# Attention with a gated MLP on one core: the reciprocals spread by VectorE instead of two DMAs, and the last exponential cut in halves

## The chip, the cores and the metric

One NeuronCore of a Trainium2 chip runs the kernel. Its engines work from queues of their own: TensorE (PE, matrix products), VectorE (DVE), ScalarE (ACT, here mainly exponentials), GpSimd (POOL) and SyncE (SP, which here issues most DMAs). They meet at semaphores. The metric is the device time of one execution in microseconds. The kernel before took 1224.72 us as the median of three executions (1223.39 to 1226.02).

## The reference

The input x has 2048 rows of 512. All is bfloat16.

```python
xn = layernorm(x)                                  # rows of 512
q  = (xn @ wq) as 32 heads of 128
p  = softmax(q @ k_cache.T * 128**-0.5)            # per head, 2048 x 2048
s  = concat(p @ v_cache) @ wo                      # 4096 -> 512
h  = relu(xn @ w1 + b1)**2                         # 512 -> 1792
out = x + s * silu(h @ w2 + b2)
```

Each of the 32 heads has its own 2048 keys and values of 128 numbers. The softmax is computed without subtracting a maximum: the exponentials are summed, and the output of a head is divided by the sum at the end.

## The kernel before

The 2048 query rows are worked in four blocks of 512. A block and a head make a unit g (128 of them: 32 heads for each block in turn), and a unit has eight steps, so there are 1024 steps (`pi`), each over 256 keys. A step computes transposed scores: `gen_scores` makes two products of 128 keys x 512 queries into `psA` (two buffers of 1024 columns), and ScalarE makes one exponential over both, into the tile `pT` (eight buffers). Two steps later the step's products with V follow, into `psO` (two banks). Between scores and V products TensorE runs one or two products of other work, from a list of jobs: projections of q for later heads, the MLP, and the output projection with `wo`, which go through the two banks of `psF` and are evicted by VectorE.

The products with V come in two kinds. In the first (`gen_pv`), pieces of 128x128 of `pT` are the stationary operand and V moves past them, with a column of ones added, so that the denominator comes out as a 129th column; 64 products of 128x129 make a head. VectorE evicts the result (`o_un`), takes the reciprocal, GpSimd scales, and a transposing DMA writes `oT`. In the second (`gen_pv_b`), V is stationary and `pT` moves; 16 products of 128x512 make a head, the result is already transposed, and ScalarE evicts it to `o_col`. The denominator then has to be found beside TensorE: GpSimd adds the two halves of a `pT` tile (`h_sum`) and VectorE reduces it with a transposing reduction (`d_part`), or VectorE reduces the `pT` tile alone at about twice the length. The partial sums of a head are summed (`d_sum`), turned in blocks of 32 (`d_row`), written to memory (`d_scr`), read back (`d_quad`), totalled and inverted (`d_rec`, on 32 partitions). The inverses are written to memory again (`r_scr`) and read back broadcast to all 128 partitions (`r_all`, two buffers). GpSimd multiplies `o_col` by `r_all` into `oT`.

Each engine's order is written out while the kernel is built. The class `_Sched` keeps a clock for each engine from a cost per instruction (`_cost`) and per DMA (`_ISSUE`). VectorE's necessary work (evictions) is placed when it arises; the rest waits in the list `quiet` with a due step, and `fill_dve` puts it wherever the planned clock leaves room. `fill_pool` does the same for GpSimd, and takes reductions off VectorE by placing an `h_sum`; `fill_sync` places the DMAs of the denominators. `ready_at` adds an allowance (`SLACK`, 1500 ns, `HALF_SLACK`, 600 ns) before what waits for a DMA or for an `h_sum`; `POOL_OWED` keeps GpSimd from taking a reduction when VectorE owes little. For each unit, `choose` takes the second kind, unless VectorE's owed work (`owed`) is above `OWED` or no `o_col` buffer of the `NOC` is in sight; the first three and last three units are always of the first kind. In the program as built, units 0-2, 33, 64, 75, 97 and 125-127 are of the first kind.

At the end of a query block `acc_gate` (the line of `_stt`, 249) multiplies the accumulated output by the gate on VectorE, four times a block. After the last unit, `tail_one` runs what is left of the output projection; the very last row tile is written from a buffer of its own, `x_t`, in pieces.

Lines of helpers carry the profile's names: L226 and L231 are the products (L231 those of the first kind), L235 ScalarE's activations, L239 tensor-tensor, L249 the fused form with a scalar, L253 copies, L257 reciprocals, L282 reductions, L286 transposing reductions, L290 the transpose in blocks of 32, L294 and L298 DMAs.

## Time and profile before

| what | value |
|---|---|
| median of three executions | 1224.72 us |
| profiled execution: time, span | 1224.72 us, 1222.9 us |
| granted TensorE clock | 1.000 |
| busy: TensorE, VectorE, ScalarE, GpSimd | 1206.5, 1083.0, 1090.7, 1066.4 us |
| exponentials | 1024, 1026 ns each |
| h_sum additions on GpSimd | 764, 1164 ns each |
| transposing reductions of h_sum, of pT | 764 of 679 ns, 180 of 1209 ns |
| scalings of o_col on GpSimd | 118, 1283 ns each, idle before them 33.5 us |
| DMA to landing: d_scr, d_quad, r_scr, r_all | 2.9, 3.3, 3.2, 3.8 us |

The page's busy time counts an engine's records without their overlap. A group's line gives the source line, engine, operation, tile written and tiles read, count, then busy time, mean length of one and the idle time of the engine just before. Products are pipelined, so their spacing is read from the starts in the timeline and not from their lengths. About one product's record in fifty is missing from the trace; a gap of 0.05 us marked "issue" in TensorE's timeline is such a place.

### The profile page before, as it was taken

To read this page: it belongs to the slowest core of one execution; us is meant where nothing else is said; L and a number is where in the kernel's file an instruction comes from. 1 tells how busy PE (TensorE), PEld (TensorE's weight loads), DVE (VectorE), ACT (ScalarE), POOL (GpSimd) and SP (SyncE) were. 2 spreads that over 40 slices of the span, in tenths; PEclk is the share of its full clock that TensorE was granted. 3 is DMA by queue.
4 is the path that set the end of the run, shared out by engine and by line. 5 is a ranking of instruction groups with operands and counts; after the bars stand their busy time and mean duration, and the time that the engine had idled before them with its cause. 6 is when DMAs were issued, how large, how long until landed. Compare 5 with 4: busy or idle time off the path is not lost.

```text
span 1222.9 us, 19101 instructions
## 1 busy us (share of the span) xinstructions
PE 1206.5 (99%) x6103; PEld 574.9 (47%) x6221; DVE 1083.0 (89%) x1874; ACT 1090.7 (89%) x1162; POOL 1066.4 (87%) x979
## 2 busy tenths in 40 slices
PE   9999999999999999999999999999999999999998
PEld 7544444444444444444454454444445444444445
DVE  4798989899999988889999988888998999988983
ACT  7899999998888999999999999998998899989984
POOL 1689999999788999999988879989898899999981
PEclk9999999999999999999999999999999999999999
DMA  9999997787787887887777898787879788878871
GB/s 217 203 236 195 207 210 148 156 172 151 166 166 153 170 186 150 152 170 157 172 168 159 168 159 174 150 166 167 167 147 158 165 176 161 155 155 159 166 153 49
DMA packets 679300, 203.53 MB, mean 166 GB/s; under 512 B 650881, under 2 KB 662913, under 8 KB 679201
## 3 DMA queue, kind: packets, MB, share of 16 engines
q1 hardware_dynamic: 677104, 198.25, 80.9%
q0 software_dynamic: 1424, 3.81, 1.0%
q8 instruction: 49, 0.80, 0.3%
q14 instruction: 51, 0.41, 0.1%
q10 hardware_dynamic: 672, 0.26, 0.1%
HBM read 128.50 MB, written 4.27 MB: 109 GB/s over the span
## 4 chain that ended last, share of the span: by engine, by line
PE 79%; DVE 14%; POOL 3%; DMA 2%; issue 1%; ACT 1%; ACTq 0%; SPq 0%; POOLq 0%; DVEq 0%
PE psA L226 29%; PE psO L226 27%; PE psF L226 20%; DVE d_part L286 8%; POOL h_sum L239 3%; PE psO L231 2%; DVE acc L249 2%; DMA d_quad<-d_scr 1%; DVE qt_sb L253 1%; DVE d_sum L282 1%; ACT pT L235 0%; DVE acc L239 0%; DVE g_all L249 0%; DMA r_scr<-d_rec 0%; POOL oT L239 0%
## 5 line engine op out<-in xcount | busy, mean ns | idle before, releaser
L235 ACT ACTIVATE pT<-psA 128x1024 bf16<-128x1024 f32 x1024 | 1036.1, 1026 | 111.8 <-PE psA L226 74.2
L239 POOL TENSOR_TENSOR h_sum<-pT 128x512 f32<-128x512 bf16 x764 | 865.1, 1164 | 48.5 <-ACT pT L235 23.6
L226 PE MATMUL psA<-qt_sb,kT 128*128 128x512 bf16 x1980 | 593.3, 379 | 4.3 <-ACT pT L235 1.2
L226 PE MATMUL psO<-pT,v_sb 128*128 128x512 bf16 x1851 | 553.5, 379 | 1.9
L286 DVE TRANSPOSE_TENSOR_REDUCE d_part<-h_sum 128x16 f32<-128x512 f32 x764 | 501.8, 679 | 34.0 <-POOL h_sum L239 32.5
L226 PEld LDWEIGHTS psA<-qt_sb,kT 128*128 128x128 bf16 x2032 | 195.1, 98 | 225.9 <-ACT pT L235 6.8
L226 PEld LDWEIGHTS psO<-pT,v_sb 128*128 128x128 bf16 x1888 | 184.7, 98 | 222.2 <-issue 0.7
L286 DVE TRANSPOSE_TENSOR_REDUCE d_part<-pT 128x32 f32<-128x1024 bf16 x180 | 217.0, 1209 | 5.7 <-ACT pT L235 5.2
L239 POOL TENSOR_TENSOR oT<-o_col,r_all 128x512 bf16<-128x512 f32 x118 | 151.3, 1283 | 33.5 <-DMA r_all<-r_scr 32.0
L226 PE MATMUL psF<-xnT,wq_sb 128*128 128x512 bf16 (+1 forms) x513 | 167.1, 374 | 1.5 <-DVE acc L239 0.6
L226 PE MATMUL psF<-wo_all,oT 128*128 128x512 bf16 x468 | 160.3, 379 | 1.5 <-DVE z_t L249 0.8
L253 DVE CAST qt_sb<-psF 128x512 bf16<-128x512 f32 (+1 forms) x130 | 85.6, 659 | 21.9 <-PE psF L226 19.9
L226 PEld LDWEIGHTS psF<-xnT,wq_sb 128*128 128x128 bf16 x520 | 50.3, 98 | 61.0 <-issue 1.4
L226 PE MATMUL psF<-xnT,w_sb 128*128 128x512 bf16 x219 | 75.7, 379 | 2.1 <-DVE h2T L249 2.0
L226 PEld LDWEIGHTS psF<-wo_all,oT 128*128 128x128 bf16 x480 | 46.9, 98 | 58.3 <-DVE z_t L249 1.3
L226 PE MATMUL psF<-w_sb,h2T 128*128 128x512 bf16 x219 | 72.4, 379 | 0.2
L235 ACT ACTIVATE o_col<-psO 128x512 f32<-128x512 f32 x118 | 69.8, 592 | 0.0
L245 DVE TENSOR_SCALAR r_t<-psF,b1f 128x512 bf16<-128x512 f32 x56 | 40.8, 728 | 12.0 <-PE psF L226 11.3
L231 PEld LDWEIGHTS psO<-v_sb,pT 128*128 128x128 bf16 x640 | 42.4, 98 | 17.6 <-ACT pT L235 0.6
L231 PE MATMUL psO<-v_sb,pT 128*128 128x129 bf16 x640 | 49.0, 220 | 0.3 <-ACT pT L235 0.3
L282 DVE TENSOR_REDUCE d_sum<-d_part 128x16 f32<-128x160 f32 (+3 forms) x118 | 46.6, 395 | 1.5
L249 DVE SCALAR_TENSOR_TENSOR h2T<-psF,b1f,r_t 128x512 bf16<-128x512 f32 x56 | 41.8, 747 | 1.7
(65 smaller groups left out, 383.4 us busy)
## 6 DMA issues: line engine op xcount, KB each, us to landing
v_sb<-in_A_v_cache_dram SPq DMA_DIRECT2D x127, 512.0 KB, 4.8
r_all<-r_scr SPq DMA_DIRECT2D x118, 256.0 KB, 3.8
wq_sb<-in_A_wq_dram SPq DMA_DIRECT2D x127, 128.0 KB, 3.4
wo_all<-in_A_wo_dram SPq DMA_DIRECT2D x4, 1024.0 KB, 5.8
w_sb<-in_B_w_dram SPq DMA_DIRECT2D x14, 256.0 KB, 4.1
x_t<-in_A_x_dram POOLq DMA_DIRECT2D x16, 128.0 KB, 3.4
kT<-in_A_k_cache_dram SPq DMA_TRANSPOSE x127, 5.1
d_scr<-d_row SPq DMA_DIRECT2D x118, 16.0 KB, 2.9
```

The source lines that it names most:

```text
L226: return e.matmul(out, lhsT, rhs, start=start, stop=stop)
L231: return e.matmul(out, lhsT, rhs, start=start, stop=stop, skip_group_check=True)
L235: return e.activation(out, in_, func, bias=bias, scale=scale)
L239: return e.tensor_tensor(out, in0, in1, op)
L245: return e.tensor_scalar(out, in0, scalar1=scalar1, scalar2=scalar2, op0=op0, op1=op1)
L249: return e.scalar_tensor_tensor(out=out, in0=in0, scalar=scalar, in1=in1, op0=op0, op1=op1)
L253: return e.tensor_copy(out, in_)
L282: return e.tensor_reduce(out, in_, axis=AX.X, op=ALU.add)
L286: return e.tensor_reduce(out, in_, axis=AX.X, op=ALU.add, apply_transpose=True)
```

## The change

Three things change together.

- The reciprocals are spread by VectorE. `d_sum` is written straight to memory in another order, every one of the 128 partitions reads the sums of all four groups of 32 rows (`d_quad`), totals and inverts them (`d_rec`), and one VectorE transpose in blocks of 32, whose source repeats each inverse 32 times, writes `r_all` (`den_spread`). `r_all` has one buffer. The turn `d_row`, the write to `r_scr` and the broadcast read go.
- The planner's numbers: `OWED` 9000, three `o_col` buffers, no allowance before `h_sum` reductions and before the scaling, no `POOL_OWED`. The memory saved or used: four buffers for the rows under normalization, a buffer of its own for the warm-up products.
- The last exponential is two of 512 columns, and the last V products are ordered by key half, the first four waiting for the first half alone.

```diff
           "wo_all": (1700, 7200), "w1_sb": (600, 5000), "w2_sb": (700, 5000), "d_scr": (530, 2200),
-          "d_quad": (530, 4200), "r_scr": (530, 2200), "r_all": (1230, 4400)}
+          "d_quad": (1230, 4200)}
...
-    OWED = 8000
-    POOL_OWED = 3500
-    HALF_SLACK = 600
+    OWED = 9000
...
-    NSL, NSW, NQS, NPT, NOT, NOC, NHS = 3, 4, 3, 8, 3 * HC, 4, 3
+    NSL, NSW, NQS, NPT, NOT, NOC, NHS = 3, 4, 3, 8, 3 * HC, 3, 3
...
-    d_sum = sb("d_sum", [P, 2, 32], F32)
-    d_row = sb("d_row", [P, 2, 32], F32)
+    d_sum = sb("d_sum", [P, 2, NBK], F32)
     d_quad = sb("d_quad", [P, 2, 4, NBK], F32)
     d_rec = sb("d_rec", [P, 2, NBK], F32)
-    r_all = sb("r_all", [P, 2, QB], F32)
-    d_scr = nc.dram_tensor("d_scr", [2, P, 32], F32, kind="Internal").ap()
-    r_scr = nc.dram_tensor("r_scr", [2, QB], F32, kind="Internal").ap()
+    r_all = sb("r_all", [P, NBK, 32], F32)
+    d_scr = nc.dram_tensor("d_scr", [2, 32, 4 * NBK], F32, kind="Internal").ap()
...
-    warm = o_bf[:, 0, 0, :]
+    warm = sb("warm", [P, P], BF16)
...
-        t_exp[pi] = E(AC, partial(_act, out=pT[:, pi % NPT, :],
-                                  in_=psA[:, s2 * 1024:(s2 + 1) * 1024],
-                                  func=ACT.Exp, scale=SM_SCALE),
-                      deps=[t, t_PV[pi - NPT] if pi >= NPT else None, t_part.get(pi - NPT)])
-
+        cuts = [0, QB, 2 * QB] if pi == NPAIR - 1 else [0, 2 * QB]
+        for c0, c1 in zip(cuts, cuts[1:]):
+            t_exp[pi] = E(AC, partial(_act, out=pT[:, pi % NPT, c0:c1],
+                                      in_=psA[:, s2 * 1024 + c0:s2 * 1024 + c1],
+                                      func=ACT.Exp, scale=SM_SCALE),
+                          deps=[t, t_PV[pi - NPT] if pi >= NPT else None, t_part.get(pi - NPT)])
+            t_exp0.setdefault(pi, t_exp[pi])
+
+    t_exp0 = {}
...
     def den_sum(g):
         m = b_no[g]
-        t_sum[m] = E(DV, partial(_reduce, out=d_sum[:, m % 2, 0:NBK],
+        t_sum[m] = E(DV, partial(_reduce, out=d_sum[:, m % 2, :],
                                  in_=d_part[:, m % 2, 0:len(t_parts[g]), :].rearrange(
                                      "p n b -> p b n")),
-                     deps=t_parts[g] + [t_row.get(m - 2) if m >= 2 else t_sum0])
-
-    def den_turn(g):
-        m = b_no[g]
-        t_row[m] = E(DV, partial(_transpose32, out=d_row[:, m % 2, :], in_=d_sum[:, m % 2, :]),
-                     deps=[t_sum[m], t_dw.get(m - 2)])
+                     deps=t_parts[g] + [t_dw[m - 2] if m >= 2 else None])
 
     def den_write(g):
         m = b_no[g]
-        t_dw[m] = S.emit_dma(SP, partial(_dma, out=d_scr[m % 2], in_=d_row[:, m % 2, :]),
-                             sl_dw[m % 2], deps=[t_row[m], t_dr.get(m - 2)])
+        dst = bass.AP(tensor=d_scr.tensor, offset=d_scr.offset + m % 2 * P * NBK,
+                      ap=[[NBK, 4], [4 * NBK, 32], [1, NBK]])
+        t_dw[m] = S.emit_dma(SP, partial(_dma, out=dst, in_=d_sum[:, m % 2, :]), sl_dw[m % 2],
+                             deps=[t_sum[m], t_dr[m - 2] if m >= 2 else None])
 
     def den_read(g):
         m = b_no[g]
-        src = bass.AP(tensor=d_scr.tensor, offset=d_scr.offset + m % 2 * P * 32,
-                      ap=[[NBK, 32], [32 * 32, 4], [1, NBK]])
-        t_dr[m] = S.emit_dma(SP, partial(_dma, out=d_quad[0:32, m % 2], in_=src), sl_dr[m % 2],
-                             deps=[t_dw[m], t_tot.get(m - 2)])
+        src = bass.AP(tensor=d_scr.tensor, offset=d_scr.offset + m % 2 * P * NBK,
+                      ap=[[0, 4], [4 * NBK, 32], [1, 4 * NBK]])
+        t_dr[m] = S.emit_dma(SP, partial(_dma, out=d_quad[:, m % 2].rearrange("p a b -> p (a b)"),
+                                         in_=src), sl_dr[m % 2],
+                             deps=[t_dw[m], t_tot[m - 2] if m >= 2 else None])
 
     def den_total(g):
         m = b_no[g]
-        t_tot[m] = E(DV, partial(_reduce, out=d_rec[0:32, m % 2, :],
-                                 in_=d_quad[0:32, m % 2].rearrange("p a b -> p b a")),
-                     deps=[t_dr[m], t_rw.get(m - 2)])
+        t_tot[m] = E(DV, partial(_reduce, out=d_rec[:, m % 2, :],
+                                 in_=d_quad[:, m % 2].rearrange("p a b -> p b a")),
+                     deps=[t_dr[m], t_spr.get(m - 2)])
 
     def den_recip(g):
         m = b_no[g]
-        t_rec[m] = E(DV, partial(_recip, out=d_rec[0:32, m % 2, :], in_=d_rec[0:32, m % 2, :]),
+        t_rec[m] = E(DV, partial(_recip, out=d_rec[:, m % 2, :], in_=d_rec[:, m % 2, :]),
                      deps=[t_tot[m]])
 
-    def rec_write(g):
+    def den_spread(g):
         m = b_no[g]
-        t_rw[m] = S.emit_dma(
-            SP, partial(_dma, out=r_scr[m % 2].rearrange("(p b) -> p b", b=NBK),
-                        in_=d_rec[0:32, m % 2, :]),
-            sl_rw[m % 2], deps=[t_rec[m], t_spr.get(m - 2)])
-
-    def rec_read(g):
-        m = b_no[g]
-        src = bass.AP(tensor=r_scr.tensor, offset=r_scr.offset + m % 2 * QB,
-                      ap=[[0, P], [1, QB]])
-        t_spr[m] = S.emit_dma(SP, partial(_dma, out=r_all[:, m % 2, :], in_=src), sl_rr[m % 2],
-                              deps=[t_rw[m], t_scale.get(m - 2)])
+        base = d_rec[:, m % 2, :]
+        spread = bass.AP(tensor=base.tensor, offset=base.offset,
+                         ap=[list(base.ap[0]), [1, NBK], [0, 32]])
+        t_spr[m] = E(DV, partial(_transpose32, out=r_all[:], in_=spread),
+                     deps=[t_rec[m], t_scale[m - 1] if m else None])
 
     def den_scale(g):
         m = b_no[g]
         t_scale[m] = tok_oT[g] = E(
             GP, partial(_tt, out=oT[:, g % NOT, :], in0=o_col[:, m % NOC, :],
-                        in1=r_all[:, m % 2, :], op=ALU.mult),
+                        in1=r_all[:].rearrange("p b i -> p (b i)"), op=ALU.mult),
             deps=[t_col[m], t_spr[m], t_wodone[g - NOT] if g >= NOT else None])
...
-              den_turn: 110}
+              den_spread: 600}
...
-        calm(first + NPR + 6, partial(den_turn, g))
...
-        sync_quiet.append(partial(rec_write, g))
-        sync_quiet.append(partial(rec_read, g))
+        calm(first + NPR + 13, partial(den_spread, g))
         pool_quiet.append(partial(den_scale, g))
...
-        slack = SLACK if fn.func in (den_total, den_read, rec_read, den_scale) else (
-            HALF_SLACK if fn.func is part_half else 0)
+        slack = SLACK if fn.func in (den_total, den_read) else 0
...
-            if (x < NHS or t_half[x - NHS] is not None) and owed(now[0]) > POOL_OWED:
+            if x < NHS or t_half[x - NHS] is not None:
...
+        if pi == NPAIR - 1:
+            order = [x for n in range(2) for x in order if x[1] == 2 * k + n]
...
-            inc = idx == len(order) - 1 or (last and g > 0 and idx == 3)
+            inc = idx == len(order) - 1 or (last and g > 0 and idx == (5 if g == NG - 1 else 3))
...
-                  deps=[t_exp[ps], t_v0[k % 2] if g == 0 else t_vfill[g], t_ones,
+                  deps=[(t_exp0 if tt == 2 * k else t_exp)[ps], t_v0[k % 2] if g == 0 else t_vfill[g], t_ones,
```

## Prediction

> **What bounds the kernel now.** I read the page first, then TensorE's waits, then its timeline, and last VectorE in the stretches where those waits lie.
>
> The head of the page:
>
> ```profile
> span 1222.9 us, 19101 instructions
> PE 1206.5 (99%) x6103; PEld 574.9 (47%) x6221; DVE 1083.0 (89%) x1874; ACT 1090.7 (89%) x1162; POOL 1066.4 (87%) x979
> ...
> PEclk9999999999999999999999999999999999999999
> ```
>
> TensorE is busy 99% of the span at full granted clock. Since overlapping records can hide stalls, I look at every wait that reached it:
>
> ```profile
> PE psF L226 <- DVE h2T L249: 2.0, 1, 2.0
> PE psA L226 <- ACT pT L235: 1.2, 3, 0.4
> PE psA L226 <- POOL mhalf L261: 1.0, 1, 1.0
> PE psF L226 <- DVE z_t L249: 0.8, 1, 0.8
> PE psF L226 <- DVE acc L239: 0.6, 1, 0.6
> PE psF L270 <- DVE xn_t L245: 0.4, 1, 0.4
> PE psF L226 <- DVE acc L253: 0.3, 1, 0.3
> PE psO L231 <- ACT pT L235: 0.3, 1, 0.3
> PE psF L226 <- DVE xnT L253: 0.2, 1, 0.2
> ```
>
> Without the start-up (mhalf, xn_t, xnT) the waits are 2.0 + 1.2 + 0.8 + 0.6 + 0.3 + 0.3 = 5.2 us in the whole run. So nothing that makes a hidden engine cheaper can win more than 5.2 us; every added matmul costs its full time; and an engine that gets late adds directly. The times of products, from the timeline of TensorE (start, length, records):
>
> ```profile
> 1197.60 0.62 PE L231 MATMUL psO<-v_sb,pT 128*128 128x129 bf16 x8
> 1198.05 0.59 PE L226 MATMUL psA<-qt_sb,kT 128*128 128x512 bf16 x2
> 1198.48 0.38 PE L226 MATMUL psF<-wo_all,oT 128*128 128x512 bf16 x1
> ```
>
> Starts count here, not lengths: eight 128x129 products take 1198.05 - 1197.60 = 0.45 us, two 128x512 take 0.43 us. Where the waits come from is seen in VectorE's busy time by stretch (the columns after the length are busy time and count of TensorE, weight loads, VectorE, ScalarE, GpSimd, then clock and DMA):
>
> ```profile
> 276.00:320.00 44.00, 41.83 (x192) 18.92 (x195) 43.90 (x60) 37.63 (x40) 39.55 (x37) 1.00 0.73 156
> ...
> 576.00:625.00 49.00, 48.69 (x270) 24.18 (x275) 47.27 (x76) 44.63 (x48) 43.13 (x40) 1.00 0.82 175
> ...
> 877.00:935.00 58.00, 57.03 (x307) 27.64 (x311) 55.35 (x92) 51.46 (x55) 49.39 (x45) 1.00 0.77 155
> ```
>
> VectorE is full there (43.90 of 44.00 us). These are the stretches with the four output gates of a query block:
>
> ```profile
> L286 DVE TRANSPOSE_TENSOR_REDUCE d_part<-h_sum 128x16 f32<-128x512 f32 x764 | 501.8, 679 | 34.0 <-POOL h_sum L239 32.5
> L249 DVE SCALAR_TENSOR_TENSOR acc<-acc,g_all 128x512 f32<-128x512 f32 x16 | 34.2, 2137 | 0.0
> L290 DVE STREAM_TRANSPOSE d_row<-d_sum 128x32 f32<-128x32 f32 x118 | 23.2, 197 | 2.4
> ```
>
> A gate means 2137 ns, and one took 4.44 us from 309.42; the wait of 2.0 us on h2T ends just behind it, at 315.40. The planner in the kernel counts about 600 ns for it, so VectorE falls behind the written order.
>
> **The change part by part.** Sums are made on the profiled execution: 1224.72 us, of which 1222.9 are span and 1.8 lie around it; that is also the median.
>
> *More heads of the first kind.* Built, the changed program has 16 heads with P as the stationary operand instead of 10 (0-2, 8, 30, 36, 45, 62, 66, 73, 95, 102, 109, 125-127; before: 0-2, 33, 64, 75, 97, 125-127). Six heads of 16 products 128x512 become 64 products 128x129: by the spacings above 8 x (0.45 - 0.43) = 0.17 us a head, 6 x 0.17 = **+1.0 us**, all on TensorE.
>
> The Trainium skill, "TensorE: Matmul & The Clock Gate", section "Back-to-back issue gap", speaks against this: it gives a sustained spacing of about 81 ns at N=128 and 131 ns at N=512, and calls the spacing of some 56 and 216 ns the isolated one. As an estimate by that page a head would go from 16 x 131 = 2.1 us to 64 x 81 = 5.2 us, and six would cost 18.5 us. This trace has 57 and 216 ns in the stream itself, so the sum goes by the row.
>
> *Reciprocals by VectorE.* Removed per head: the 32-wide turn d_row (197 ns), the write to r_scr and the broadcast read into r_all (3.2 and 3.8 us to landing, issued by SP; 236 issues go). No TensorE wait names a DMA, so their removal gains 0 there; GpSimd's 32.0 us of waiting for r_all go, but they lie beside other work. Total and reciprocal now run on 128 partitions with the same free size; I keep their 221 and 224 ns. The read of the sums brings 32 KB instead of 8: it landed in 3.3 us, the 256 KB one in 3.8, so 0 to 0.5 us later for a reduction that waited 12.3 us in 13 of 118 cases. Added: 112 transposes 128x512. The nearest row is the transposing reduction over 512 float elements, 679 ns; ends are 197 ns (32 elements) and 1209 ns (1024 elements). I take 0.68 us, 76 us in all.
>
> *VectorE's load.* Against these 76 us stand 48 fewer reductions of 1209 ns (58), all 118 turns (23), six each of sum, total and reciprocal (5), and 12 more evictions of 0.42 plus six small reciprocals (+6): net -4 us of 1083. By place it is not even. Summing the row durations over each program's written order and taking 0.915 of it (neighbours overlap: 1083 busy of 1183 summed), heads 28-47 need 172 us instead of 180, 60-79 172 instead of 175, 92-111 167 instead of 175, against 183 to 188 of TensorE; heads 112-127 need 134 instead of 128, against 141. Room remains everywhere; the rows allow the 5.2 us to fall or stay.
>
> *Where the evictions stand.* With P stationary, the output is evicted by VectorE, and the next head's first product needs the bank. In the trace:
>
> ```profile
> 331.47 0.62 PE L231 MATMUL psO<-v_sb,pT 128*128 128x129 bf16 x8
> 331.92 0.59 PE L226 MATMUL psA<-qt_sb,kT 128*128 128x512 bf16 x2
> 332.35 0.38 PE L226 MATMUL psF<-xnT,wq_sb 128*128 128x512 bf16 x1
> 332.57 0.59 PE L226 MATMUL psO<-pT,v_sb 128*128 128x512 bf16 x2
> ```
>
> The half bank is done at about 331.70, the next user starts 0.87 us later, and the copy takes 0.42: VectorE may come 0.4 us late, no more. Before, the four such heads in the middle had their last output gate 24 or more VectorE instructions back (34, 24, 25; one stands behind a gate of the other kind), and VectorE arrived 0, 0.98, 1.35 and 0 us early. In the changed order the copy of head 30 stands 4 instructions behind a gate and that of head 62 9 behind, and in six of the ten the spread comes within two places before the copy. A gate exceeds its plan by 2137 - 600 = 1.5 us, at most 3.8. Bounds: 0 (VectorE early everywhere, or catching up elsewhere by as much) to 2 x 3.8 + 8 x 0.7 (one spread late) = 13 us; below nothing the other stalls can give at most 5.2. I take 1.5 - 0.4 = 1.1 us for each of the two, and 0.1 for the other eight: **+3.0 us**, and leave the 5.2 us as they are.
>
> *New coupling.* r_all is single: the spread waits for GpSimd's scaling of the head before, and behind it in VectorE's queue are the evictions that TensorE waits for. GpSimd's scaling waits for the spread, and behind it are the h_sum additions, for which VectorE already waited 32.5 us in 85 cases (0.38 each). The planner's 600 ns allowance for that wait and its rule for sparing GpSimd go. Bounds: -2 (the waits for r_all held h_sum up) to 112 x 0.38 = 43 us on VectorE, of which the middle's free tenth takes most; I take 0 and keep the rest as a rival. Three instead of four o_col buffers: ScalarE never waited with four (0.0 us idle before them), and the chain that frees them loses two DMAs, so 0.
>
> *The end.* The last exponential (1026 ns) becomes two of about 592 (the 128x512 copy on ScalarE). The last half ends 2 x 592 - 1026 = 0.16 us later, but only 4 of the last 8 products (0.23 us) follow it: 0.16 - 0.23 = -0.07; at best the whole 0.27 us wait goes. I take **-0.1 us**. Own buffers for warm-up and first rows, four row loads together, no d_sum memset (144 ns on GpSimd): 0, off every chain shown.
>
> Sum: 1224.72 + 1.0 + 3.0 - 0.1 = **1228.6 us**.
>
> **The rivals.** *Relief (faster).* The same stalls come from VectorE's lateness, and it has 3 to 8 us less to do in each gate stretch. If all 5.2 us go: 1224.72 + 1.0 - 0.1 - 5.2 = 1220.4. It decides from stalls below about 1.9 us in all (5.2 + 1.0 - 0.1 - 1.9 > 0.2%). Against it: a gate of 4.44 us remains possible, and evictions move next to gates.
> *Nothing to see.* Stalls stay near 5: 1224.72 + 0.9 = 1225.6.
> *Coupling.* If waits of 0.38 us at 112 spreads, or spreads of 1.2 us (+59 us), fill VectorE, its 89% becomes 93 to 94% and the gate stretches run over: a loss of some 2 us at each of the six heavy spots plus the above, 1228.6 + 12 = 1240. For it: VectorE full in the three windows; against: less work planned there.
>
> **How the numbers follow.** Late evictions 0.40, nothing to see 0.25, coupling 0.20, relief 0.15. About 0.2% (2.45 us) is what can be told from no change: below 1222.3 is faster (0.15), above 1227.2 slower (0.60). The range reaches from most of the relief case, 1221, to the coupling case, 1239; the likeliest case alone is 1227 to 1233.
>
> **What would show it.** Right: TensorE's waits name o_un near heads 30 and 62, the spread takes about 0.68 us, spacings stay 57 and 216 ns, total waits about 8 us. Wrong: waits of VectorE on GpSimd's scaling in most heads, ScalarE waiting before o_col, or TensorE's waits under 3 us.

## The result, and the profile after

The changed kernel took 1221.26 us as the median of six executions (1220.44 to 1222.51). The kernel before, run beside it on the same chip, took 1225.01 us (six, 1223.39 to 1226.02). The ratio is 0.9972 with a 95% interval of 0.9959 to 0.9985: faster by 0.28%, a little more than the 0.2% that can be told from no change. The prediction was 1228.6 us and slower; the kernel became faster, and the time lies just inside the predicted range of 1221 to 1239.

The head of the page of the changed kernel (profiled execution 1222.51 us):

```profile
span 1220.7 us, 19228 instructions
PE 1205.7 (99%) x6386; PEld 587.2 (48%) x6509; DVE 1077.0 (88%) x1820; ACT 1088.6 (89%) x1157; POOL 1067.2 (87%) x978
...
PEclk9999999999999999999999999999999999999999
```

Nothing in the shares tells the difference: TensorE is again at 99% and full granted clock, VectorE has 6 us less. TensorE's waits tell more (waiting engine, line, released by: total us, times, longest us):

```profile
PE psO L226 <- DVE o_un L253: 1.9, 1, 1.9
PE psO L270 <- DMA kT<-in_A_k_cache_dram: 1.2, 2, 0.6
PE psA L226 <- ACT pT L235: 1.0, 1, 1.0
PE psA L226 <- POOL mhalf L261: 1.0, 1, 1.0
```

Before, these were nine lines with 5.2 us outside the start-up. Now 2.9 us are left (o_un and pT; kT and mhalf belong to the start-up), and the h2T, z_t and acc waits are gone. Summing the starts of TensorE's products over each trace gives the balance of the two spans: first 128x512 product 0.28 us later, products +1.06 us, stalls between them 3.77 instead of 7.39 us (-3.62; this counts short gaps that the list of waits leaves out), the end +0.07. The difference of the stalls is firmer than the two sums, which depend on the spacing that is taken as undisturbed. Together -2.21 us, 1222.9 to 1220.7.

VectorE in the three stretches with output gates that the prediction used (busy time and count of TensorE, weight loads, VectorE, ScalarE, GpSimd; clock; DMA share and GB/s):

```profile
276.00:320.00 44.00, 43.74 (x248) 21.95 (x252) 40.48 (x62) 39.24 (x41) 38.22 (x36) 1.00 0.76 139
576.00:625.00 49.00, 48.74 (x271) 24.23 (x275) 45.20 (x71) 44.60 (x48) 44.39 (x41) 1.00 0.75 144
877.00:935.00 58.00, 56.64 (x306) 27.75 (x311) 53.80 (x87) 51.93 (x55) 52.72 (x49) 1.00 0.70 145
```

VectorE has 3.42, 2.07 and 1.55 us less in them. The groups that the prediction priced, by form (line, engine, operation, tiles, shapes, count; busy us, mean ns; idle us before them):

```profile
L286 DVE TRANSPOSE_TENSOR_REDUCE d_part<-h_sum 128x16 f32<-128x512 f32 x764 | 506.5, 686 | 33.1 <-POOL h_sum L239 30.5
L290 DVE STREAM_TRANSPOSE r_all<-d_rec 128x512 f32<-128x512 f32 x112 | 76.8, 686 | 0.5
L249 DVE SCALAR_TENSOR_TENSOR acc<-acc,g_all 128x512 f32<-128x512 f32 x16 | 26.0, 1624 | 0.0
L282 DVE TENSOR_REDUCE d_rec<-d_quad 128x16 f32<-128x64 f32 x112 | 25.9, 231 | 3.4 <-DMA d_quad<-d_scr 3.4
```

The spread takes 686 ns, as estimated. The gates are shorter (1624 instead of 2137 ns, still 0.65 to 3.22 us each). The last line holds what the prediction passed over. Its counterpart, in VectorE's waits before and after:

```profile
DVE d_rec L282 <- DMA d_quad<-d_scr: 12.3, 13, 2.4
```

```profile
DVE d_rec L282 <- DMA d_quad<-d_scr: 3.4, 3, 1.5
```

VectorE stood still 12.3 us for the sums to come back from memory; now it is 3.4. The read of the sums is issued by SyncE, and the longest of SyncE's waits before for one of the two DMAs that the change removes was

```profile
SPq L294 <- DMA r_scr<-d_rec: 108.3, 69, 3.1
```

that is, SyncE stood 108.3 us until r_scr had landed, so that it could issue the read into r_all, and whatever stood behind it in its queue, the writes of other heads' sums among it, waited too. This line is gone after; SyncE now stands for the sums themselves:

```profile
SPq L294 <- DVE d_sum L282: 157.7, 60, 5.1
SPq L294 <- DMA d_scr<-d_sum: 118.0, 54, 4.0
```

It is there when they come. The lengths of SyncE's DMA records, summed over its timeline, fall from 862 us before to 647 us.

How a late read reaches TensorE can be followed in the changed kernel itself, because one of its two profiles has such a case and the other, taken in a later run of the same kernel, has not. SyncE, VectorE and TensorE in the first (start, length, operation, tiles; in brackets the idle time before):

```profile
84.03 5.49 SPq L298 DMA_TRANSPOSE kT<-in_A_k_cache_dram  x1
89.56 0.56 SPq L294 DMA_DIRECT2D d_quad<-d_scr  x1
```

```profile
92.80 0.26 DVE L282 TENSOR_REDUCE d_rec<-d_quad 128x16 f32<-128x64 f32 x1 [1.50 <-DMA d_quad<-d_scr]
...
96.74 0.75 DVE L253 COPY o_un<-psO 128x258 f32<-128x258 f32 x2
```

```profile
97.30 0.59 PE L226 MATMUL psO<-pT,v_sb 128*128 128x512 bf16 x2 [1.85 <-DVE o_un L253]
```

and SyncE in the second profile of the same kernel:

```profile
82.31 3.66 SPq L298 DMA_TRANSPOSE kT<-in_A_k_cache_dram  x1
86.02 0.56 SPq L294 DMA_DIRECT2D d_quad<-d_scr  x1
```

In the first a key transpose started 1.72 us later and held SyncE 1.83 us longer, so the read of the sums was issued at 89.56 instead of 86.02. VectorE stood 1.50 us for it, the output copy of unit 8 behind it in VectorE's queue ended late, and TensorE waited 1.85 us for the bank. In the second profile the copy came at 94.40 and TensorE did not wait. No DMA is named in TensorE's wait, and yet a DMA made it.

The kernel before has the whole chain, r_scr included, behind its 0.8 us of z_t. SyncE, VectorE and TensorE there:

```profile
945.98 1.25 SPq L294 DMA_DIRECT2D r_scr<-d_rec  x1
950.19 0.34 SPq L294 DMA_DIRECT2D r_all<-r_scr  x1
950.58 0.43 SPq L294 DMA_DIRECT2D d_scr<-d_row  x1
...
954.94 2.12 SPq L294 DMA_DIRECT2D d_quad<-d_scr  x1
```

```profile
947.11 0.17 DVE L290 STREAM_TRANSPOSE d_row<-d_sum 128x32 f32<-128x32 f32 x1
...
960.15 0.25 DVE L282 TENSOR_REDUCE d_rec<-d_quad 32x16 f32<-32x64 f32 x1 [0.94 <-DMA d_quad<-d_scr]
...
962.25 0.64 DVE L249 SCALAR_TENSOR_TENSOR z_t<-psF,g_all 128x512 f32<-128x512 f32 x1
```

```profile
962.95 0.39 PE L226 MATMUL psF<-wo_all,oT 128*128 128x512 bf16 x1 [0.84 <-DVE z_t L249]
```

The sums were ready at 947.28 us. SyncE had issued r_scr by 947.23 and stood for its landing, so that the read into r_all went at 950.19 and the write of the sums only at 950.58. VectorE then stood 0.94 us for the sums, made no pause from there to z_t, and TensorE waited 0.84 us. The two stalls on acc (0.6 and 0.3 us) also follow a wait for d_quad (1.60 and 1.80 us) without a pause of VectorE in between.

The longest stall of the kernel before, 2.0 us on h2T, is not of this kind:

```profile
309.42 4.44 DVE L249 SCALAR_TENSOR_TENSOR acc<-acc,g_all 128x512 f32<-128x512 f32 x1
...
314.61 0.73 DVE L249 SCALAR_TENSOR_TENSOR h2T<-psF,b1f,r_t 128x512 bf16<-128x512 f32 x1
```

```profile
315.40 0.39 PE L226 MATMUL psF<-xnT,w_sb 128*128 128x512 bf16 x1 [1.96 <-DVE h2T L249]
```

VectorE waited for d_quad at no time between 206 and 800 us, and between 274 and 316 us for nothing that the profile shows. It was late by its own work, the last of it a gate of 4.44 us. So of the 5.2 us of stalls before, 1.7 hang directly on late sums and 2.0 on the gates; the 1.5 us on pT were not followed.

### The profile page after: what moved, and what is told of

Its sections match the earlier page's. It is cut to its first block, busy times and chain, and to the rows that moved or that the text cites. A ratio compares the mean times of both kernels' runs of the same rounds, so it can differ in the third digit from the quotient of the medians.

```text
span 1220.7 us, 19228 instructions
## 1 busy us (share of the span) xinstructions
PE 1205.7 (99%) x6386; PEld 587.2 (48%) x6509; DVE 1077.0 (88%) x1820; ACT 1088.6 (89%) x1157; POOL 1067.2 (87%) x978
## 4 chain that ended last, share of the span: by engine, by line
PE 94%; DVE 2%; POOL 1%; issue 1%; DMA 1%; ACT 0%; SPq 0%; ACTq 0%; POOLq 0%; DVEq 0%
PE psA L226 35%; PE psO L226 31%; PE psF L226 24%; PE psO L231 4%; DVE d_part L286 1%; POOL h_sum L239 1%; DVE acc L249 0%; DMA kT<-in_A_k_cache_dram 0%; ACT pT L235 0%; PE psA L231 0%; DMA d_quad<-d_scr 0%; DVE h2T L249 0%; POOL oT L239 0%; DVE r_t L245 0%; DVE r_all L290 0%
## 5 line engine op out<-in xcount | busy, mean ns | idle before, releaser
L286 DVE TRANSPOSE_TENSOR_REDUCE d_part<-h_sum 128x16 f32<-128x512 f32 x764 | 506.5, 686 | 33.1 <-POOL h_sum L239 30.5
L226 PE MATMUL psO<-pT,v_sb 128*128 128x512 bf16 x1759 | 525.8, 379 | 3.8 <-DVE o_un L253 1.9
L226 PEld LDWEIGHTS psO<-pT,v_sb 128*128 128x128 bf16 x1792 | 175.3, 98 | 213.3 <-issue 3.5
L239 POOL TENSOR_TENSOR oT<-o_col,r_all 128x512 bf16<-128x512 f32 x112 | 144.6, 1291 | 32.1 <-DVE r_all L290 31.9
L286 DVE TRANSPOSE_TENSOR_REDUCE d_part<-pT 128x32 f32<-128x1024 bf16 x132 | 159.1, 1212 | 4.4 <-ACT pT L235 4.0
L231 PEld LDWEIGHTS psO<-v_sb,pT 128*128 128x128 bf16 x1024 | 68.1, 98 | 28.8 <-ACT pT L235 0.4
L226 PEld LDWEIGHTS psF<-xnT,wq_sb 128*128 128x128 bf16 x520 | 50.2, 98 | 60.0 <-issue 0.7
L231 PE MATMUL psO<-v_sb,pT 128*128 128x129 bf16 x1024 | 78.7, 220 | 0.2
L290 DVE STREAM_TRANSPOSE r_all<-d_rec 128x512 f32<-128x512 f32 x112 | 76.8, 686 | 0.5
L235 ACT ACTIVATE o_col<-psO 128x512 f32<-128x512 f32 x112 | 66.3, 592 | 0.0
L282 DVE TENSOR_REDUCE d_sum<-d_part 128x16 f32<-128x144 f32 (+3 forms) x112 | 43.1, 385 | 1.1
```

Of the source, the lines that this page charges most:

```text
L226: return e.matmul(out, lhsT, rhs, start=start, stop=stop)
L231: return e.matmul(out, lhsT, rhs, start=start, stop=stop, skip_group_check=True)
L235: return e.activation(out, in_, func, bias=bias, scale=scale)
L239: return e.tensor_tensor(out, in0, in1, op)
L282: return e.tensor_reduce(out, in_, axis=AX.X, op=ALU.add)
L286: return e.tensor_reduce(out, in_, axis=AX.X, op=ALU.add, apply_transpose=True)
```

## The experiments

Ratios are to the kernel before, run beside each kernel on the same chip; versions that ran on different chips are compared by their ratios. A profile shows one execution, a time is the median of several. Four theories stood against each other for the gain: **lighter VectorE** (A in the expectations, the relief rival: the choice of heads and the smaller load take the stalls away), **queue** (B: the two DMAs held up SyncE's queue and with it the sums), **gates** (D: the output gates make VectorE late, and the change happens to shorten them), and **order** (C: a different written order that happens to fit).

### The parts on their own

The last exponential in halves, put into the kernel before:

```diff
+        cuts = [0, QB, 2 * QB] if pi == NPAIR - 1 else [0, 2 * QB]
+        for c0, c1 in zip(cuts, cuts[1:]):
+            t_exp[pi] = E(AC, partial(_act, out=pT[:, pi % NPT, c0:c1], ...
...
-                  deps=[t_exp[ps], ...
+                  deps=[(t_exp0 if tt == 2 * k else t_exp)[ps], ...
```

> The kernel before with one part of the change alone: the last exponential in two halves and the last V products ordered by key half. Nothing else in the written order differs. From the two profiles the wait at the last V products goes from 0.27 to 0.09 us, so every theory expects 0.1 to 0.3 us less, 1224.8 us against 1225.0 of before, too little to tell in the time; the wait in the profile tells it.

1221.72 us beside 1222.02, ratio 0.9998 (0.9985 to 1.0011). The wait of the last V products fell from 0.27 to below 0.1 us in the profile, as far as so small a thing can be read; in the time it can't be measured. The halves are not the gain.

Fewer heads of the second kind in the kernel before, so that VectorE has less to do:

```diff
-    OWED = 8000
+    OWED = 6000
```

> The kernel before with OWED 6000 instead of 8000: 18 heads of the first kind instead of 10, the two DMAs of the reciprocals kept. VectorE's row sums fall to 169, 164, 164 and 123 us in heads 28-47, 60-79, 92-111 and 112-126 (before: 180, 175, 175, 128; the changed kernel: 172, 172, 167, 134). Theory A (VectorE's lighter load in the gate stretches ended the stalls): stalls fall as in the changed kernel, the 8 heads cost 1.4 us, so 1221 to 1223 us. Theory B (the two DMAs that went, by SyncE's queue, the traffic and their landing): stalls stay and the 1.4 us come on top, 1225.5 to 1227 us. Theory C (any new written order moves the stalls by some us, this change drew a good one): anywhere in 1221 to 1229.

1223.30 us, ratio 1.0011 (1.0002 to 1.002). VectorE's busy time fell from 1083.0 to 1040.7 us and TensorE still waited: the lines ahead of the start-up's are 1.4 us for pT, 1.3 for h2T, 1.1 for acc. A load lighter by 4% did not take the stalls away; the time moved by about the 1.4 us that the expectation counts for the products of eight more heads of the first kind. In the other direction, in the changed kernel:

```diff
-    OWED = 9000
+    OWED = 14000
```

> The changed kernel with OWED 14000 instead of 9000: 10 heads of the first kind instead of 16, the spread on VectorE kept. VectorE's row sums rise to 188, 184, 179 and 136 us in the four stretches, more than before had. Theory A: stalls come back, 5 us or more of them, and the time is 1224 to 1230 us although 1.0 us of products goes. Theory B: the time stays or falls by the 1.0 us, 1220 to 1221.5 us. Theory C: anywhere in 1220 to 1229.

1238.95 us (four executions), ratio 1.0145 (1.0131 to 1.0159). With 10 heads of the first kind VectorE goes to 1133.6 us (92%), and TensorE's longest line becomes

```profile
PE psA L226 <- ACT pT L235: 13.5, 19, 2.8
```

VectorE frees the pT buffers by its reductions; ScalarE waits 22.2 us for them (`d_part` in its list of waits), and TensorE for ScalarE. No theory had expected so much. So the six additional heads of the first kind are no source of gain but what pays for the spread: without them this kernel loses 17 us to the kernel before (1238.95 - 1222.02).

The same 16 heads of the first kind, in the kernel before:

```diff
-            choose(g, FIRST_B <= g < NG - 3 and owed(pi) < OWED and (m < NOC or m - NOC in t_dr))
+            choose(g, g not in [0, 1, 2, 8, 30, 36, 45, 62, 66, 73, 95, 102, 109, 125, 126, 127])
```

> The kernel before with the list of heads of the first kind fixed to the 16 of the changed kernel; its planner places the rest by its own rules, and the reciprocals go by DMA. Products are then the same 1185.2 us in the middle as in the changed kernel. If the choice of heads made the gain (A), 1219.5 to 1221 us and a ratio of 0.996 to 0.998. If the way of the reciprocals made it (B or E), stalls stay at 5 us or more: 1223 to 1226 us, ratio 0.9995 to 1.002, runs spread over 3 us or more.

1228.16 us, ratio 1.0037 (1.002 to 1.0054); stalls 13.0 us counted from the starts, VectorE's wait for d_quad 21.9 us in 16 cases, GpSimd's for r_all 50.2. The choice of heads, with the DMAs left in, makes the kernel slower. **Lighter VectorE**, as far as it is the choice and number of heads, falls; less work at the gates alone is another matter, as the next runs show.

### The gates

In these two the output gate multiplies 64 of the 512 columns, so the output is gated only there:

```diff
+def _stt_thin(e, out, in0, scalar, in1, op0, op1):
+    n = 64
+    return e.scalar_tensor_tensor(out=out[:, 0:n], in0=in0[:, 0:n], ...
...
-        t_ug[jt] = E(DV, partial(_stt, out=acc[:, qt, :], in0=acc[:, qt, :], scalar=0.5,
+        t_ug[jt] = E(DV, partial(_stt_thin, out=acc[:, qt, :], in0=acc[:, qt, :], scalar=0.5,
```

> The kernel before with the 16 output gates done on 64 of their 512 columns, planned as if whole, so that the written order of every engine is that of before; the gate's product is left out on the other 448 columns. If the gates' length beyond their plan is what makes VectorE late (theory A, and my reading of the profile before), the waits of TensorE on VectorE go, 3.7 of 5.2 us, and the time is 1221 to 1222 us. If the DMAs or the order by itself did it (B, C), the waits stay at the same places and the time is 1224 to 1225 us.

1218.35 us, ratio 0.9976 (0.9966 to 0.9987), some 3.7 us less (1222.02 - 1218.35), with the DMAs in place: nearly the gain of the change. In the profile all stalls behind the start-up are gone but one (the definition above moves the lines by six):

```profile
PE psA L226 <- POOL mhalf L267: 1.0, 1, 1.0
PE psO L231 <- ACT pT L235: 0.3, 1, 0.3
```

SyncE stood for r_scr as long as before (105.6 us in 67 cases), but VectorE's waits for d_quad fell to 6.6 us in 6. The standing by itself does not make a stall; it can where VectorE has little time to spare, as at z_t above.

> The changed kernel with the 16 output gates done on 64 of 512 columns, planned as if whole; the gate's product is left out on the other 448 columns. In the kernel before this took all stalls but 0.3 us away and gave 0.9976. If the gates cause what is left of the changed kernel's stalls too (D), its time falls to 1218 to 1219.5 us, within 0.1% of the thin-gate kernel before, the 1.0 us of the six heads on top. If its stalls have another source (the evictions beside the spread, as I forecast, or the coupling by the single r_all), TensorE's waits stay at 2 to 3 us and the time at 1220 to 1221 us.

1218.84 us beside 1223.93, ratio 0.9959 (0.9946 to 0.9972); the whole changed kernel, run again beside it,

> The changed kernel once more, on the chip of this call, because the kernel before took 1222.0 us on the chip of the first four experiments and 1225.0 us beside the changed kernel. If its gain is its own (theory A: fewer stalls by design), it stays at a ratio of 0.996 to 0.9985 to before. If the stalls of before vary by chip and run by as much as the gain (theory D: both kernels have the same source of stalls, the gates, and its size is drawn anew), the ratio comes nearer to 1, 0.998 to 1.001.

took 1220.20 us (1220.01 to 1220.66), ratio 0.997 (0.9958 to 0.9982). So 448 of the gates' 512 columns cost some 3.7 us before and 1.4 us after (1220.20 - 1218.84). Thinner gates and the change remove much the same stalls, and their gains do not add. The gates are therefore a part of the cause in the kernel before, and the change did not touch their size; why they took 1624 ns in its profile and 2137 before was not tested.

Two other ways to help the gates were tried in both kernels. The gate on GpSimd instead of VectorE (the factor 0.5 goes into z_t), in the kernel before and, later, in the changed kernel:

```diff
-                calm(step + 16, partial(acc_gate, j, qt))
+                pool_quiet.append(partial(acc_gate, j, qt))
...
-        t_ug[jt] = E(DV, partial(_stt, out=acc[:, qt, :], in0=acc[:, qt, :], scalar=0.5,
-                                 in1=g_all[:, jt % TPB, :], op0=ALU.mult, op1=ALU.mult),
+        t_ug[jt] = E(GP, partial(_tt, out=acc[:, qt, :], in0=acc[:, qt, :],
+                                 in1=g_all[:, jt % TPB, :], op=ALU.mult),
```

> The kernel before with the 16 output gates on GpSimd as plain products, planned as such; the factor 0.5 goes into the term z (z, the bias and the scale of tanh are halved or doubled to match). The whole computation is kept. VectorE loses 16 x 2.14 = 34 us and what it was late by, GpSimd gains 16 x 1.15 = 18 us. If the gates' length on VectorE is the source of the stalls, the waits of TensorE on VectorE go and the time comes to 1217.5 to 1219.5 us, below both kernels. If GpSimd, 87% busy, becomes late in its place, ScalarE waits for h_sum more than the 6.5 us of before and the time stays at 1221 to 1224 us.

1224.61 us beside 1223.93, ratio 1.0003 (0.9992 to 1.0014): no gain. The waits for d_quad rose to 21.3 us in 20 cases and new stalls came at 97 to 226 us and at 476, most of them behind such a wait (1.27 us at 223 ahead of the stall at 226, for one).

> The changed kernel with the output gates on GpSimd (13 heads of the first kind, -0.5 us; the whole computation is kept). In the kernel before this won nothing, as the reads of the sums came late there. With the queue free: 1218.5 to 1220 us if the gates are all that is left; 1220.5 to 1223 us if GpSimd becomes late instead.

1219.23 us (1218.88 to 1223.23), ratio 0.996 (0.9943 to 0.9977). Nothing of the computation is left out, and this is the lowest median of such a version; its interval overlaps that of the changed kernel, so that it beats it by 1 us is likely and not shown. With the DMAs in, the same edit gave nothing.

The planner told a price nearer the measured one (1950 ns; the mean was 2137 ns before), in both:

```diff
+    elif f is _stt and _in_sbuf(k["in0"]) and k["out"].tensor.name == "acc":
+        n = 1950
```

> The kernel before with the planner told that an output gate takes VectorE some 2.1 us instead of 0.6; nothing else. It then makes 15 heads of the first kind (+0.9 us of products) and places the reductions by a truer clock. If the stalls come from the plan's error (A and D), they fall from some 5 us to 1 to 2 and the time is 1219.5 to 1221.5 us. If they come from the gate itself, which takes between 0.6 and 4.4 us as it happens to meet GpSimd, a truer mean changes little: 1221.5 to 1224 us.

1223.94 us, ratio 1.0007 (0.9998 to 1.0016), waits for d_quad 13.2 us. TensorE waits for no eviction any more, but 2.4 us for pT.

> The changed kernel with the planner told that an output gate takes some 2.1 us (17 heads of the first kind, +0.2 us). The changed kernel has 1.4 us between it and its thin-gate form. If the plan's error makes these, 1219 to 1220 us, the best so far; if the gate's meeting with GpSimd does, 1220.2 to 1221.5 us.

1220.95 us, ratio 0.9962 (0.9947 to 0.9978), the changed kernel's own. Planning the gate is worth nothing measurable in either.

### Is it the written order?

The change redraws the order of every engine. Two variants of the changed kernel with orders of their own: the old two row buffers,

```diff
-    x_ln = sb("x_ln", [P, TPB, D], BF16)
-    xn_t = sb("xn_t", [P, TPB, D], BF16)
+    x_ln = sb("x_ln", [P, 2, D], BF16)
+    xn_t = sb("xn_t", [P, 2, D], BF16)
```

> The changed kernel with the row buffers of the normalization as before (two rows and two normalized rows instead of four each), everything else as changed: the control of the next run, which needs the memory. TensorE's and ScalarE's order are that of the changed kernel but for four lines. If that part of the change is worth nothing, as I costed it: 1219.5 to 1221 us, ratio 0.996 to 0.998, the runs within 1.5 us of each other.

1220.65 us (1220.30 to 1221.03), ratio 0.9973 (0.9961 to 0.9984); and the old allowance before the reductions of h_sum, by which 17 heads are of the first kind instead of 16:

```diff
-        slack = SLACK if fn.func in (den_total, den_read) else 0
+        slack = SLACK if fn.func in (den_total, den_read) else (
+            600 if fn.func is part_half else 0)
```

> The changed kernel with one planner number of before back: 600 ns of allowance ahead of the reductions of h_sum (17 heads of the first kind instead of 16, other orders everywhere). If a kernel that spreads on VectorE is fast and steady under another written order too (B or E), 1219.5 to 1222 us, runs within 1.5 us. If the changed kernel just drew a good order (C), this one draws anew: 1219 to 1226 us, stalls of 2 to 7 us in the profile, though again steady from run to run.

1220.74 us (1220.58 to 1220.96), ratio 0.9974 (0.9962 to 0.9985). Both gain what the change gains. **Order** falls. The first also says that the own buffers for the rows are worth nothing, and it is the control of what follows.

### The two DMAs put back

The write to r_scr and the broadcast read issued again by SyncE behind each reciprocal, into a buffer that nobody reads. The orders of the four other engines, and of SyncE's other DMAs, are those of the control in the traces, and the planner's clock doesn't see the new DMAs:

```diff
+    r_dummy = sb("r_dummy", [P, QB], F32)
...
+        sync_quiet.append(partial(rec_write, g))
+        sync_quiet.append(partial(rec_read, g))
```

> The control with the two DMAs of each head put back on SyncE, reading the reciprocals and writing them broadcast into a buffer that nobody uses; the orders of TensorE, VectorE, ScalarE and GpSimd are those of the control to the line. Theory B (their traffic and SyncE's time cost the kernel before some us, and make its time vary by 5 us from run to run): the time rises by 1 to 4 us over the control, and the runs spread over 3 us or more. Theory E (only the waiting of GpSimd for their landing matters, as nobody waits here): within 0.5 us of the control, runs within 1.5 us.

1247.24 us (six, 1243.60 to 1254.57), ratio 1.0197 (1.0166 to 1.0228), against 0.9973 for the control; the expectation had been 1 to 4 us. Stalls of TensorE rose from 1.6 to 25.4 us. VectorE's and SyncE's waits in this run:

```profile
DVE d_rec L282 <- DMA d_quad<-d_scr: 49.0, 36, 4.6
```

```profile
SPq L294 <- DMA r_scr<-d_rec: 73.9, 48, 2.9
SPq L294 <- DVE d_rec L257: 70.4, 34, 4.3
```

No work depends on these DMAs but the reuse of d_rec two heads later, and VectorE's waits name r_scr nowhere. They cost 26.6 us (1247.24 - 1220.65). SyncE stops for the reciprocal (70.4 us; 37.6 in the control, for other DMAs) and for r_scr's landing, and the sums behind it come late; that this standing is what costs, the next run tests. It is more than they can have cost in the kernel before, whose planner places work by them: there all stalls behind the start-up are 5.2 us.

The same DMAs issued two (write) and three (read) heads later, when what they wait for has long been met (SyncE's list of waits then names r_scr nowhere); d_rec gets four buffers for it, and the other orders stay those of the control:

```diff
     def den_read(g):
...
+        if m >= 3:
+            rec_read(b_heads[m - 3])
+        if m >= 2:
+            rec_write(b_heads[m - 2])
```

> As the run with the DMAs put back, same bytes and same number, but each is issued two or three heads later, just behind the read of the sums of another head, when what it reads has long been there: SyncE's queue does not stand for it. Orders of the four other engines again as in the control. If the traffic or the issue time is what cost 26 us, the time stays above 1235 us. If the standing queue is it (SyncE waited 108 us in 69 places for r_scr in the kernel before, and the read of the sums behind it came late), the time comes back to 1220.5 to 1222 us, VectorE's wait for d_quad back to below 5 us, and the runs lie within 1.5 us.

1226.74 us (1223.63 to 1227.80), ratio 1.0011 (1.0 to 1.0023). This lies between the two expectations: 1.9% of the time, the standing of the queue, went, and 0.4% stayed, with waits for d_quad of 11.0 us where below 5 had been expected. Two runs ask what stayed, traffic or issue. First the read cut to 16 of its 512 columns, with the same number of DMAs:

```diff
-                      ap=[[0, P], [1, QB]])
-        t_rr[m] = S.emit_dma(SP, partial(_dma, out=r_dummy[:], in_=src), sl_rr[m % 2],
+                      ap=[[0, P], [1, 16]])
+        t_rr[m] = S.emit_dma(SP, partial(_dma, out=r_dummy[:, 0:16], in_=src), sl_rr[m % 2],
```

> The changed kernel (two row buffers) with the write to r_scr and the read issued two and three heads later, as in the run where they were unwaited, but the read brings 16 of the 512 reciprocals to each partition: the same DMAs are issued, 28 MB less is moved. What the unwaited DMAs left, about 0.4% of the time, is either traffic or issue. Traffic: the time falls back to that of the changed kernel, 1220.5 to 1222 us, with d_quad waits of 2 to 4 us. Issue: it stays near 1225 to 1228 us, with d_quad waits near the 11.0 us of that run.

1225.12 us beside 1222.96, ratio 1.0014 (1.0003 to 1.0024): with 28 MB less the loss is the same. Then the late write alone, without the read:

```diff
-        if m >= 3:
-            rec_read(b_heads[m - 3])
```

> The same with the late write to r_scr alone, without any read: half of the added DMAs, hardly any traffic. Traffic: 1220.5 to 1221.5 us, as the changed kernel. Issue: about half of the loss, 1222.5 to 1225 us, with d_quad waits of 5 to 8 us.

1222.11 us, ratio 0.9988 (0.9977 to 0.9999): about 0.15% of the 0.4%. The time lies between the two expectations, and the interval touches that of the control, so this step alone is not clear of noise; the step to the small read is. It is not the bytes but the number of DMAs. Whether a further DMA costs by its issue on SyncE or by its packets, of which the small read has as many as the whole one (676471 in all in both profiles), these runs do not separate. The steps side by side, with the summed length of SyncE's DMA records in each profile:

| version | ratio to before | SyncE's DMA records | VectorE's waits for d_quad |
|---|---|---|---|
| control, no DMAs added | 0.9973 | 643 us | 1.5 us in 3 |
| late write alone | 0.9988 | 701 us | 5.8 us in 4 |
| late write, small read | 1.0014 | 775 us | 7.9 us in 8 |
| late write, whole read | 1.0011 | 801 us | 11.0 us in 10 |
| both at once, unplanned | 1.0197 | 881 us | 49.0 us in 36 |

The profiled executions of the three late versions took 1223.6 us each, so the waits belong to these and the ratios to the medians. The longest of the waits fall at 160 to 174 us, where the control has none; with the whole read TensorE's 1.4 us on z_t at 170 follow a wait of 3.22 us at 163. The waits of the small and the whole read, as VectorE's list of waits has them:

```profile
DVE d_rec L282 <- DMA d_quad<-d_scr: 7.9, 8, 2.2
```

```profile
DVE d_rec L282 <- DMA d_quad<-d_scr: 11.0, 10, 3.2
```

The record of one such late DMA is only 0.44 to 0.52 us long in the mean, and it lands in 2.2 to 3.8 us. The Trainium skill, "DMA: Bandwidth & Descriptors", section "Issuing engines are not separate DMA queues", says that the time a sequencer needs to initiate a DMA is usually small relative to the DMA itself. That agrees, and it misleads here: what counts is not its share of the DMA but which other DMA stands behind it in the queue.

One attempt to mend the kernel before by its planner alone, 3000 ns of allowance before the broadcast read:

```diff
-        slack = SLACK if fn.func in (den_total, den_read, rec_read, den_scale) else (
+        slack = SLACK if fn.func in (den_total, den_read, den_scale) else (
...
+        if fn.func is rec_read:
+            slack = 3000
```

> The kernel before with an allowance of 3000 instead of 1500 ns ahead of the broadcast read of the reciprocals, so that SyncE reaches it later and stands less for the landing of r_scr (12 heads of the first kind instead of 10, +0.3 us of products). If the standing queue is the source, SyncE's 108 us fall by more than half, VectorE's wait for d_quad falls below 5 us, and the time falls to 1220 to 1222.5 us. If not, 1222.5 to 1225 us.

1231.13 us (six, 1229.92 to 1234.66), ratio 1.0058 (1.0038 to 1.0078). The expectation failed. SyncE's standing for r_scr halved (54.6 us instead of 108.3), but the waits for d_quad stayed at 12.9 us and the order came out new, with 12 first-kind heads and VectorE waiting 45.9 us for h_sum (32.5 before). Of its larger stalls, one of 2.40 us follows a wait for d_quad (3.68 us) and one of 1.70 us a wait for h_sum (3.48 us). So half the standing less brought nothing: how long SyncE stands is not by itself what the time goes by in the kernel before.

## Why the prediction was wrong

*The step that failed* is in "Reciprocals by VectorE": "No TensorE wait names a DMA, so their removal gains 0 there". Without the removal there is no gain: with the other parts of the change kept (but for the row buffers, which are worth nothing), putting the DMAs back, without any wait to stand for, brought the ratio from 0.9973 to 1.0011, and the waits for them, unplanned, cost another 1.9%. The prediction had both halves of it on the table: VectorE's 12.3 us for d_quad in 13 cases, which it cited only to argue that a larger read would be hidden, and SyncE, of which it counted that "236 issues go" without looking at SyncE's own waits. A wait list names the last releaser. TensorE waited for z_t, VectorE was late with z_t because it had stood for d_quad, and d_quad was late because SyncE had stood for r_scr.

*"Leave the 5.2 us as they are"* follows from that and fell with it: 2.9 us are left in the profile shown, and in the second profile 1.0 us in the list of waits (1.7 counted from the starts). The prediction's reading of the longest stall, 2.0 us on h2T behind a gate of 4.44 us, was right, and this stall went too. No wait for d_quad leads to it, so what took it away was not singled out: in its stretch the changed order gives VectorE 3.42 us less to do.

*Late evictions, +3.0 us*, was wrong too, and is the term that made the forecast "slower": of the 7.3 us between forecast and time (1228.6 - 1221.26), 3.0 are this term and some 3.6 the stalls. The copy of head 30 stood 4 places behind a gate as predicted, but that gate took 0.68 us and VectorE was 0.72 us early; at head 62 the gate 9 places back took 2.28 us, VectorE had no time to spare, and TensorE did not wait. The gates meant 1624 ns, not 2137. The one wait for o_un is at unit 8, far from any gate, in one profile of two, and came from a late DMA.

*The added products, +1.0 us*, was right: +1.06 us from the starts. The spacings are the old ones:

```profile
1203.21 0.59 PE L226 MATMUL psA<-qt_sb,kT 128*128 128x512 bf16 x2
1203.65 0.62 PE L231 MATMUL psO<-v_sb,pT 128*128 128x129 bf16 x8
1204.10 0.59 PE L226 MATMUL psA<-qt_sb,kT 128*128 128x512 bf16 x2
```

1203.65 - 1203.21 = 0.44 us for two products 128x512, 0.45 for eight 128x129. The estimate of +18.5 us by the sustained spacings of the Trainium skill, "TensorE: Matmul & The Clock Gate", section "Back-to-back issue gap", does not hold here: the measured +1.06 us stand against it.

*The spread at 0.68 us* was right (0.686), *the last exponential at -0.1* agrees with the profile and is too small for the time, *the row buffers at 0* too: the version with the old ones is as fast. Three o_col buffers and the warm-up had no run of their own; ScalarE again never sat idle before o_col (0.0 us).

*The rivals.* Relief named almost the measured time (1220.4 against 1221.26), and its condition, stalls below about 1.9 us behind the start-up, is met in the second profile. (The sum in brackets behind that condition has the 1.0 - 0.1 with the wrong sign; 5.2 - 1.9 - 0.9 = 2.4 us, so the 1.9 stands.) Its reason was at most half right: a smaller load of VectorE alone (the 18 heads) or the new heads alone brought nothing, but less work at the gates did. That its number came so near is in part luck. Coupling did not show: GpSimd waited 31.9 us for the spread in place of 32.0 for r_all, VectorE's waits for h_sum went from 32.5 to 30.5. It was given a chance of 0.20, relief 0.15; SyncE's list of waits, had it been read, spoke for a gain.

What stays open: how much of the kernel before's 3 to 4 us is late sums and how much the gates. In its profile 1.7 us follow late sums and 2.0 a long gate, and thinner gates gained as much as the change with the DMAs in place. The late versions give a price of 0.4% for the DMAs in an order that was planned without them; the early one is an upper bound. No run plans the changed kernel with the DMAs counted, and the allowance before the scaling, `POOL_OWED` and the number of `o_col` buffers were not tried alone in the kernel before; in the changed kernel they stayed as changed in the runs that put the DMAs back, and did not save the gain.

## What to carry to other kernels

When an engine at the bound waits for another, follow that engine's own waits one step back, and the issuing queue's one step further, before a DMA is called free, and do it stall by stall, since two stalls of one profile can have two causes; a DMA that nobody waits for can still cost through the one queued behind it. A round trip through memory in a chain that repeats for each head should be ranked by the waits that its issuing queue must stand, and issued only when they are met. Two repairs that draw on the same few microseconds of stalls do not add: thinner gates gained 3.7 us before the change and 1.4 after it.

## What the runs showed of the hardware

- What DMAs cost that nothing waited for, on SyncE's queue in this kernel: 110 writes of 2 KB moved the ratio from 0.9973 to 0.9988 (the intervals touch), 109 reads with them to 1.0014 at 8 KB each and 1.0011 at 256 KB. The size did not show.
- The issue record of the 127 key transposes on SyncE is shorter when fewer bytes move beside them: mean 2716 ns before, 2224 in the control, 2235 with the late write, 2234 with the small read, 2474 with the whole read. The bytes are not all of it: the same whole read, issued early, gives 2708. Here the traffic does show, and yet the time hardly moves with it.
- A gate on VectorE with both inputs in SBUF has a length that its size does not settle: 64 columns mean 952 ns (203 to 2460), 512 columns 1624 ns (650 to 3218) after and 2137 ns (642 to 4443) before. The Trainium skill, "GPSIMD Engine Reference", section "8. Key points", names contention of GpSimd with VectorE instructions of two SBUF inputs; the spread of the times fits that, and no run here took GpSimd's work away to show it.
- Variation from run to run: the later runs of the changed kernel, its thin gates, its two row buffers, its allowance and its planned gates (5 to 12 executions each) spread over 0.4 to 0.7 us; its first runs spread over 2.1 us and the gates on GpSimd over 4.4. The kernel before beside them spread over 5 to 11 us, the late DMAs over 3.8 to 6, and every other version with the DMAs over some 3.5 us or more. Most of the unsteadiness comes along with these DMAs; why was not tested.
